# A GFNet and ReGLU block on one core: four buffers of rounded rows, a shorter first fetch, W_down's maxima later, and ScalarE's background work queued by units

## The chip, the cores and the metric

The kernel runs on one core of one Trainium2 chip. The metric is the time of one execution on the device in microseconds (us). Before the change three runs took 489.46 to 490.03 us, with a median of 489.92 us. What is asked is how this median moves.

## What is computed

The input x has S = 2048 rows of D = 448 numbers. A layer norm of each row feeds two branches, and their sum is added to x:

```python
xn = layernorm(x)                                  # over D, eps 1e-5
X  = rfft2(xn) * (w_r + 1j * w_i)                  # spectral branch
y  = irfft2(X, s=(S, D))
gate, up = xn @ W_gate, xn @ W_up                  # D x F, F = 1792
h  = where(gate > 0, gate, 0) * up
return x + y + h @ W_down                          # F x D
```

All arrays are in f32.

## The kernel before

TensorE works on fp16 operands. Each f32 operand is split in a rounded high part and a low part (the rest, rounded again), and a product of two such operands is three matmuls: high by high, high by low, low by high.

**Tiles and loops.** The hidden dimension F is cut in 14 *f-slices* of 128, in three groups of 5, 5 and 4. The rows are cut in four *chunks* q of 512, each of four *blocks* of 128 rows (block number n2 = q + 4j); the chunks are worked on in the order 0, 2, 1, 3. A *unit* `gu` (`gu_unit`) computes gate and up of one f-slice for one chunk: 20 full passes of 128x512 (L589, `gu_full`) and 4 half passes (L596, `gu_half`). The last 64 of the 448 input columns of gate and of up fill only half of TensorE's rows, so the half passes of two successive units (*mates*) stand together. Two units fit in PSUM (`gu`, two buffers). ScalarE and VectorE then make h from gate and up and split it (`gu_post`, L621 to L625). When the units of a group are done for a chunk, four `dn` follow, one for each block: 15 matmuls of 128x448 (12 in the last group), L637, two buffers in PSUM, each added to the output rows xy by VectorE (L643).

**Rows.** For each block the statistics of the layer norm are taken (`ln_stats`, L197 and L200) and the reciprocal deviations of a chunk's four blocks worked out together (`ln_rstd`, L208 to L214). `ln_xn` (L233) writes the normalized row xn, `ln_hi` (L242) rounds it into the buffer tt with two small copies on GpSimd, `ln_lo` (L254, L255) puts the low part beside it. Then tt is transposed into T, which the units read: in the opening by TensorE (`ln_tp`, L267) with the eviction `ln_ev` (L273 on ScalarE, L275 on VectorE), later by four transposing DMAs for each chunk (`ln_dma`, L261). There are two buffers tt, used in turn, and two of xn.

**Weights.** A *slab* is the gate half or the up half of one f-slice: 128x512 in f32, loaded by L175 into one of six buffers wst. `w_sq` takes its sum of squares (ScalarE, L525, then a sum over the partitions on GpSimd, L528), `w_scale` makes a power of two from it (VectorE, L537 to L541), and `w_hl` rounds the slab (ScalarE, L548) and takes the low part (VectorE, L549). W_down goes the same way for a whole group: `load_wd` (L185), `wd_max` (VectorE, L554, and GpSimd, L556), `wd_scale` (L563 to L570), `wd_split` (ScalarE, L575, and VectorE, L576).

**Order.** The opening is written by hand for TensorE, VectorE, ScalarE and SyncE (`manual_schedule`, L832 to L897): the loads of the first chunk's four blocks, seven slabs and the identity, chunk 0's layer norm, and f-slice 0 on the first half of the chunk's columns (blocks 0 and 4), then on the second half (blocks 8 and 12). Behind it a scheduler with a simulated timeline orders the instructions of each engine. Weight work hangs on units by the table `at`: `sched(gslot(s, n), ...)` puts a step n units ahead of the unit s. The spectral branch is a background list whose pieces are issued between units. What is issued with a unit may not be ordered ahead of an anchor, the last VectorE instruction of an earlier unit (`after`, `issue_after`). Each engine runs its instructions in the order so found, and SyncE (SP) issues all DMAs named here from one queue.

Of the kernel before, what the change touches and what calls it, by code (L numbers as in the profile page):

```python
# [116 lines left out]
def tile_gfnet_reglu(ctx: ExitStack, tc: tile.TileContext, x, xr, wgu, wd, wf, ident, c_fd, c_fm, c_im, c_id, out):  # L117
# [37 lines left out]
    def ft(shape, dt, name, bufs=1):  # L155
        return fwd_pool.tile(shape, dt, name=name, bufs=bufs)
# [8 lines left out]
    def load_xr(n2):  # L165

        xr_b[n2] = free.pop(0)
        xr_t[n2] = xr_b[n2].rearrange("p g c k -> p (g c k)")[:, 0:D]
        nc.sync.dma_start(xr_t[n2], xrv[:, n2, :])
# [9 lines left out]
    def load_wn(eng=nc.sync):  # L179
        if wq:  # L180
            load_w(*wq.pop(0), eng)
# [10 lines left out]
    mv = {}  # L192
# [8 lines left out]

    rst = {}

    def ln_rstd(q):
        w = ft([128, 6, 4], F32, "rs", 2)
        vv, r0, t, r, nm, sd = (w[:, i] for i in range(6))
        m = mv[q]
        A.activation(sd, m[:, :, 1], AF.Sqrt, bias=eps)  # L208
        V.tensor_scalar(vv, m[:, :, 1], 1e-5, None, op0=OP.add)
        V.reciprocal(r0, sd)  # L210
        V.scalar_tensor_tensor(t, r0, -0.5 * 2048, vv, op0=OP.mult, op1=OP.mult)
        V.tensor_tensor(t, t, r0, op=OP.mult)
        V.scalar_tensor_tensor(r, t, 1.5 * 2048, r0, op0=OP.add, op1=OP.mult)
        V.scalar_tensor_tensor(nm, m[:, :, 0], -1.0, r, op0=OP.mult, op1=OP.mult)  # L214
        for j in range(4):
            rst[q, j] = r[:, j:j + 1], nm[:, j:j + 1]

    xn, tt = {}, {}
    tts = [ft([128, 8, 128], F16, f"tt{i}") for i in range(2)]
    for t in tts:  # L220
        G.memset(t[:, 7, 48:64], 0.0)

    def new_tt(n2):
        tt[n2] = tts[state.setdefault("tn", 0) % 2]
        state["tn"] += 1

    def ln_xn(n2, act=True):
        xn[n2] = ft([128, D], F32, "xn", 2)
        r, nm = rst[n2 % 4, n2 // 4]
        if act:  # L230
            A.activation(xn[n2], xr_t[n2], AF.Identity, scale=r, bias=nm)
        else:
            V.tensor_scalar(xn[n2], xr_t[n2], r, nm, op0=OP.mult, op1=OP.add)  # L233
# [18 lines left out]
    def ln_lo(n2):  # L252
        x, t = xn[n2], tt[n2].rearrange("p a b -> p (a b)")
        V.tensor_tensor(t[:, 512:896], x[:, 0:384], t[:, 0:384], op=OP.subtract)  # L254
        V.tensor_tensor(t[:, 448:512], x[:, 384:448], t[:, 384:448], op=OP.subtract)  # L255

    tp, last = {}, {}

# [10 lines left out]
    def ln_ev(n2, a0, a1, act):  # L269
        q, j = n2 % 4, n2 // 4  # L270
        o = Tq[q][:, a0:a1, 128 * j:128 * (j + 1)]
        if act:
            A.activation(o, tp[n2][:, a0:a1], AF.Copy)  # L273
        else:
            last["V"] = V.tensor_copy(o, tp[n2][:, a0:a1]).ins  # L275

# [233 lines left out]


    wt, wdt, wsc = {}, {}, {}
    SMALL = V
    NR = max(GROUPS)


# [13 lines left out]
    def w_scale(f, gs=(0, 1)):  # L530
        m = state["wm", f]
        g = slice(gs[0], gs[-1] + 1)
        n = len(gs)
        sc = mt([128, 2, 2], F32, "wsc", 4)
        e = eg[:, f, g]
        E = SMALL
        E.tensor_scalar(e.bitcast(U32), m[:, 1, g].bitcast(U32), 1, EXPMASK, op0=OP.logical_shift_right,  # L537
                        op1=OP.bitwise_and)
        E.tensor_scalar(sc[:, 0, 0:n], e, TINY * SQ * 2.0 ** -64, 2.0 ** 50 / SQ, op0=OP.max, op1=OP.mult)
        V.reciprocal(sc[:, 1, 0:n], sc[:, 0, 0:n])  # L540
        E.tensor_scalar(e, e, TINY * SQ * 2.0 ** -64, 2.0 ** 64 / SQ, op0=OP.max, op1=OP.mult)  # L541
        for i, k in enumerate(gs):
            wsc[f, k] = sc[:, 1, i:i + 1]

# [73 lines left out]

    def gu_post(f, q):
        g1 = mt([128, 512], F32, "g1", 3)  # L620
        A.activation(g1, hps[f, q][:, 0, :], AF.Relu, scale=2.0 ** -22)  # L621
        last["V"] = V.scalar_tensor_tensor(g1, hps[f, q][:, 1, :], 2.0 ** -22, g1, op0=OP.mult, op1=OP.mult).ins  # L622
        h = ht[f, q] = mt([128, 2, 512], F16, "h", NR + 2)
        A.activation(h[:, 0, :], g1, AF.Copy)  # L624
        V.tensor_tensor(h[:, 1, :], g1, h[:, 0, :], op=OP.subtract)  # L625
# [167 lines left out]
    def sched(i, fn, *a):  # L793
        at.setdefault(max(i, -1), []).append((fn, a))
# [4 lines left out]
    def gslot(i, back):  # L799
        n = gpos[i] - back  # L800
        return gus[n] if n >= 0 else -1
# [11 lines left out]
            sched(gus[2 + 5 * c], load_x, q + 4 * j)  # L813
    for g, fs in enumerate(groups):
        s = max(i for i in gus if i < first["dn", g])
        sched(gslot(s, 5), wd_max, fs)
        sched(gslot(s, 3), wd_scale, g, fs)
        for i, f in enumerate(fs):
            sched(gslot(s, 3 - i // 2), wd_split, f, i)
        for f in (groups[g + 1] if g + 1 < len(groups) else ()):  # L820
            sched(s, load_wd, f)

# [9 lines left out]
    with tc.manual_schedule(engines={mybir.EngineType.PE, mybir.EngineType.DVE, mybir.EngineType.Activation,  # L832
                                     mybir.EngineType.SP}):
        A.activation(mt([128, 1], F32, "root"), eps, AF.Sqrt)
        for j in range(4):
            load_xr(4 * j)
        load_wn()
        load_wn()
        nc.sync.dma_start(id_t, ident)
        for _ in range(4):  # L840
            load_wn()
        G.memset(warm, 0.0)
        wps = psum.tile([128, 512], F32, name="dn", bufs=2)
        keep_warm(NWARM)
        for j in range(4):
            ln_stats(0, j)
        w_sq(0, (0,))
        ln_rstd(0)
        w_sq(0, (1,))
        for n2 in (0, 4):  # L850
            new_tt(n2)
        ln_hi(0, True)
        w_scale(0, (0,))
        ln_xn(0, False)
        ln_xn(4, False)
        ln_tp(0, (0, 1, 2))
        keep_warm(2)
        ln_lo(0)
        w_hl(0, 0)
        ln_hi(4)  # L860
        ln_tp(4, (0, 1, 2))
        keep_warm(2)
        ln_ev(0, 0, 3, True)
        ln_ev(4, 0, 3, True)
        ln_lo(4)
        gu_open(0, 0)
        gu_full(0, 0, (0,), half[0], True, False, seq1)
        ln_tp(0, (4, 5, 6, 3, 7))
        ln_tp(4, (4, 5, 6, 3, 7))
        w_scale(0, (1,))  # L870
        ln_ev(0, 3, 8, False)
        ln_ev(4, 3, 8, False)
        gu_full(0, 0, (0,), half[0], False, False, seq2)
        for n2 in (8, 12):
            new_tt(n2)
        ln_xn(12, False)
        w_hl(0, 1)
        ln_xn(8, True)
        ln_hi(8)
        gu_full(0, 0, (1,), half[0], True, False, seq1 + seq2)  # L880
        ln_lo(8)
        w_sq(1, (0,))
        ln_hi(12)
        w_sq(1, (1,))
        free.extend(xr_b.pop(4 * j) for j in range(4))
        ln_lo(12)
        ln_tp(8, (0, 1, 2, 4, 5, 6, 3, 7))
        w_scale(1)
        ln_ev(8, 0, 8, True)
        ln_tp(12, (0, 1, 2, 4, 5, 6, 3, 7))  # L890
        ln_ev(12, 0, 8, False)
        gu_full(0, 0, (0,), half[1], False, False, seq1 + seq2)
        w_hl(1, 0)
        w_hl(1, 1)
        gu_full(0, 0, (1,), half[1], False, False, seq1 + seq2)
        for j in range(4):
            load_xr(CHUNKS[1] + 4 * j)  # L897
# [10 lines left out]
    took = lambda u: 4.6 if u[0] == "gu" else 0.57 * len(groups[u[1]])  # L908
    nu = sum(took(u) for u in units[RAMP:]) - BGEND
    rate = nbg / nu  # L910
    anchors = [last["V"]]

    @contextmanager
    def after(i):
        with tc.issue_after(anchors[max(0, len(anchors) - 1 - i)]):
            yield

    for i, u in enumerate(units):
        is_gu = u[0] == "gu"
        if is_gu:  # L920
            _, g, f, q = u
            run_bg(until=marks["T", q])
            gu_unit(f, q, (mates.get(u) or (0, 0, None, None))[2:])
        else:
            _, g, n2, _ = u
            dn_mm(groups[g], n2)
        with after(LAG):
            for fn, a in at.get(i, []):
                with tc.high_priority(offset=200):
                    fn(*a)  # L930
            for v in units[i + 1:i + 1 + AHEAD]:
                if v[0] == "gu":
                    run_bg(until=marks["T", v[3]])
            run_bg(amount=took(u) * rate if i >= RAMP else 0.0)
        if is_gu:
            with tc.high_priority(offset=400):
                gu_post(f, q)
        else:
            if g == len(groups) - 1 and pos[0] < len(bg):
                run_bg(until=len(bg))  # L940
            with tc.high_priority(offset=400):
                dn_post(g, n2)
            if g == len(groups) - 1:
                store(n2)
        anchors.append(last["V"])
    run_bg(until=len(bg))


# [43 lines left out]
```

## Time and profile before

| | |
|---|---|
| median of three runs | 489.92 us |
| the profiled execution | 489.91 us |
| its span | 488.0 us |
| mean granted TensorE clock | 0.986 |
| TensorE busy | 468.8 us, 96% |
| VectorE busy | 383.7 us, 79% |
| ScalarE busy | 171.5 us, 35% |
| DMA | 38.71 MB in all |

The span is the time from the first to the last instruction of the core; all times in the trace count from its start. The engines are called PE (TensorE), DVE (VectorE), ACT (ScalarE), POOL (GpSimd) and SP (SyncE, which issues the DMAs); PEld is TensorE's loading of weights. A row such as `L589 MATMUL gu<-T,wt 128*128 128x512 f16 x20` names line, operation, the tile written, the tiles read, shape, type and count. The brackets at a row's end hold the idle time of the engine ahead of it and what ended it.

### The profile page before, as it was taken

The numbers are of one execution on the slowest core, as the hardware profiler recorded it, in microseconds if no ns is written. First come the engines' busy times: TensorE is split into PE (matmuls) and PEld (weight loads), VectorE is DVE, ScalarE is ACT, GpSimd is POOL, SyncE is SP. The second block draws the span as 40 slices with busy tenths as digits, with TensorE's granted clock in tenths as the row PEclk, the third lists the DMA queues.
The fourth block names the chain that finished last, engine by engine and source line by source line (L and its number), as shares of the span: only waits on it lengthen the run. The fifth ranks groups of instructions, "written<-read, shape, count | busy, mean of one in ns | idle before, by whom it ended". The sixth has DMA issues, their size and how long they took to land.

```text
span 488.0 us, 7692 instructions
## 1 busy us (share of the span) xinstructions
PE 468.8 (96%) x2896; PEld 245.3 (50%) x2896; DVE 383.7 (79%) x928; ACT 171.5 (35%) x340; POOL 26.4 (5%) x61
## 2 busy tenths in 40 slices
PE   6798599999999999999999999999999999999997
PEld 2543145555545555544444444444465655656653
DVE  5897149759893978999999999999999576776642
ACT  4768124322421764243023122262254234323310
POOL 1304000300200000000000000010000000000000
PEclk9899599999999999999999999999999999999999
DMA  7999400500510345432111102010000100010022
GB/s 258 385 375 251 89 0 18 118 17 4 122 29 0 122 123 174 133 107 91 39 40 43 35 19 59 24 40 1 0 23 24 60 12 21 23 69 32 21 75 95
DMA packets 35294, 38.71 MB, mean 79 GB/s; under 512 B 15302, under 2 KB 31430, under 8 KB 35256
## 3 DMA queue, kind: packets, MB, share of 16 engines
q1 hardware_dynamic: 35256, 38.21, 26.1%
q8 instruction: 23, 0.38, 0.3%
q14 instruction: 15, 0.12, 0.1%
HBM read 31.38 MB, written 3.67 MB: 72 GB/s over the span
## 4 chain that ended last, share of the span: by engine, by line
PE 75%; DVE 8%; DMA 5%; ACT 1%; issue 1%; POOL 0%; SPq 0%; ACTq 0%; DVEq 0%; POOLq 0%
PE gu L589 40%; PE dn L637 23%; PE fx L476 4%; PE fx L504 3%; PE gu L596 3%; DMA wmx<-in_wf 2%; DVE small L399 1%; PE fx L287 1%; DVE wt L549 1%; PE fx L329 1%; DMA T<-tt 1%; DMA fm<-in_c_fm 1%; PE fx L331 1%; PE fx L333 1%; DVE wdm L554 1%
## 5 line engine op out<-in xcount | busy, mean ns | idle before, releaser
L589 PE MATMUL gu<-T,wt 128*128 128x512 f16 (+1 forms) x1140 | 257.5, 379 | 1.7 <-DVE T L275 1.5
L589 PEld LDWEIGHTS <-wt 128*128 128x128 f16 x1140 | 110.1, 98 | 133.6 <-issue 15.0
L637 PE MATMUL dn<-wdt,h 128*128 128x448 f16 x672 | 135.8, 352 | 1.1 <-DVE xy L643 1.0
L637 PEld LDWEIGHTS <-h 128*128 128x128 f16 x672 | 65.5, 98 | 62.3 <-issue 2.4
L621 ACT ACTIVATE g<-gu 128x512 f32<-128x512 f32 x56 | 33.3, 594 | 98.4 <-PE gu L596 59.0
L622 DVE SCALAR_TENSOR_TENSOR g<-gu,g 128x512 f32<-128x512 f32 x56 | 38.4, 685 | 21.1 <-ACT g L621 20.8
L624 ACT ACTIVATE h<-g 128x512 f16<-128x512 f32 x56 | 35.1, 628 | 43.7 <-DVE g L622 43.2
L643 DVE SCALAR_TENSOR_TENSOR xy<-dn,dsc,xy 128x448 f32<-128x448 f32 x48 | 32.5, 680 | 20.5 <-PE dn L637 20.3
L625 DVE TENSOR_TENSOR h<-g,h 128x512 f16<-128x512 f32 x56 | 38.4, 686 | 7.9 <-ACT h L624 7.6
L463 DVE SCALAR_TENSOR_TENSOR vt<-y,fsc,vt 128x456 f16<-128x456 f32 x16 | 11.0, 691 | 18.6 <-ACT vt L457 18.6
L596 PE MATMUL gu<-T,wt 64*128 64x512 f16 x112 | 17.4, 390 | 8.1 <-DMA T<-tt 7.1
L548 ACT ACTIVATE wt<-wst,wsc 128x512 f16<-128x512 f32 x28 | 18.6, 711 | 16.7 <-DVE wsc L540 15.9
L476 PEld LDWEIGHTS <-vt 128*128 128x128 f16 x384 | 22.7, 98 | 3.4
L476 PE MATMUL fx<-im,vt 128*128 128x128 f16 x384 | 23.9, 219 | 0.0
L525 ACT ACTIVATE junk<-wst 128x512 bf16<-128x512 f32 x28 | 17.5, 623 | 17.7 <-DMA wst<-in_wgu 17.5
L457 ACT ACTIVATE vt<-y,fsc 128x456 f16<-128x456 f32 x16 | 10.8, 675 | 27.5 <-PE fx L476 22.5
L549 DVE SCALAR_TENSOR_TENSOR wt<-wst,wsc,wt 128x512 f16<-128x512 f32 x28 | 20.3, 743 | 0.0
L492 ACT ACTIVATE pgh<-pg 114x512 f16<-114x512 f32 x16 | 10.1, 630 | 27.9 <-DVE pg L490 27.9
L528 POOL PARTITION_ALL_REDUCE wm<-wm x16 | 8.7, 544 | 180.2 <-ACT junk L525 180.2
L504 PE MATMUL fx<-idc_t,pgh 114*128 114x112 f16 (+1 forms) x192 | 16.4, 236 | 0.0
L319 ACT ACTIVATE Xh<-X 128x456 f16<-128x456 f32 x16 | 9.1, 576 | 19.2 <-DVE X L317 12.2
L243 POOL COPY tt<-tt 128x48 f16<-128x48 f16 x16 | 10.8, 675 | 83.8 <-ACT tt L242 83.1
(102 smaller groups left out, 457.1 us busy)
## 6 DMA issues: line engine op xcount, KB each, us to landing
wst<-in_wgu SPq DMA_DIRECT2D x28, 256.0 KB, 4.7
wmx<-in_wf SPq DMA_DIRECT2D x16, 228.0 KB, 2.6
wf<-in_wf SPq DMA_DIRECT2D x16, 228.0 KB, 2.4
y<-in_xr SPq DMA_DIRECT2D x16, 224.0 KB, 4.8
xy<-in_x SPq DMA_DIRECT2D x16, 224.0 KB, 4.8
out<-xy SPq DMA_DIRECT2D x16, 224.0 KB, 1.9
wdst<-in_wd SPq DMA_DIRECT2D x14, 224.0 KB, 4.2
fm<-in_c_fm SPq DMA_DIRECT2D x16, 192.0 KB, 2.6
```

What stands on the lines that cost most here:

```text
L476: P.matmul(o, v[:, h, w], m[:, c, :], start=(i == 0), stop=(i == 5), skip_group_check=True)
L504: P.matmul(ps[:, o0:o1], h[:, a, i, :], idc_t[:, b, c0:c0 + o1 - o0], start=(j == 0 and i < 3), stop=True, skip_group_check=True)
L548: A.activation(w[:, 0:4, :], st, AF.Copy, scale=sc)
L549: V.scalar_tensor_tensor(w[:, 4:8, :], st, sc, w[:, 0:4, :], op0=OP.mult, op1=OP.subtract)
L589: last["P"] = P.matmul(hps[f, q][:, g, cs], wt[f, g][:, a, :], Tq[q][:, b, cs], start=(start and i == 0), stop=(stop and i == len(seq) - 1 ...
L596: m = P.matmul(hps[f, q][:, g, 0:512], wt[f, g][rows, 7, :], Tq[q][rows, b, :], start=start, stop=not start).ins
L621: A.activation(g1, hps[f, q][:, 0, :], AF.Relu, scale=2.0 ** -22)
L622: last["V"] = V.scalar_tensor_tensor(g1, hps[f, q][:, 1, :], 2.0 ** -22, g1, op0=OP.mult, op1=OP.mult).ins
L624: A.activation(h[:, 0, :], g1, AF.Copy)
L625: V.tensor_tensor(h[:, 1, :], g1, h[:, 0, :], op=OP.subtract)
L637: last["P"] = P.matmul(ps[:, 0:D], ht[f, q][:, a, js], wdt[f][:, b, :], start=(i == 0), stop=(i == n - 1)).ins
L643: last["V"] = V.scalar_tensor_tensor(xy[:, n2, :], dps[n2][:, 0:D], dsc[:, g:g + 1], xy[:, n2, :], op0=OP.mult, op1=OP.add).ins
```

## The change

- The buffers of rounded rows tt are four, used in turn. xn has no buffers of its own now; `ln_xn` takes one from the list `free` of the y buffers, and `ln_lo` gives it back.
- `ln_rstd` can work on some of a chunk's blocks (`js`), and its scratch tile rs has three buffers for two.
- The opening loads blocks 0 and 4, a slab, the identity, a slab, blocks 8 and 12, and four slabs; it takes statistics and rstd of blocks 0 and 4 first and those of 8 and 12 behind the first passes of f-slice 0; the square of the second slab is later, and both squares of f-slice 1 stand in one call.
- W_down's maxima, scales and splits are one unit later (for group 0 the maxima two).
- The anchors hold a ScalarE instruction also (`last["A"]`): what is issued with a unit may not be ordered ahead of the last ScalarE instruction of an earlier unit either.
- The alias SMALL of VectorE is gone; the instructions are the same.

```diff
-    def ln_rstd(q):
-        w = ft([128, 6, 4], F32, "rs", 2)
-        vv, r0, t, r, nm, sd = (w[:, i] for i in range(6))
-        m = mv[q]
+    def ln_rstd(q, js=(0, 1, 2, 3)):
+        n = len(js)
+        w = ft([128, 6, 4], F32, "rs", 3)
+        vv, r0, t, r, nm, sd = (w[:, i, 0:n] for i in range(6))
+        m = mv[q][:, js[0]:js[-1] + 1, :]
...
-    tts = [ft([128, 8, 128], F16, f"tt{i}") for i in range(2)]
+    tts = [ft([128, 8, 128], F16, f"tt{i}") for i in range(4)]
...
-        tt[n2] = tts[state.setdefault("tn", 0) % 2]
+        tt[n2] = tts[state.setdefault("tn", 0) % 4]
...
-        xn[n2] = ft([128, D], F32, "xn", 2)
+        xn_b[n2] = free.pop(0)
+        xn[n2] = xn_b[n2].rearrange("p g c k -> p (g c k)")[:, 0:D]
...
         V.tensor_tensor(t[:, 448:512], x[:, 384:448], t[:, 384:448], op=OP.subtract)
+        free.append(xn_b.pop(n2))
...
-            A.activation(o, tp[n2][:, a0:a1], AF.Copy)
+            last["A"] = A.activation(o, tp[n2][:, a0:a1], AF.Copy).ins
...
-        A.activation(g1, hps[f, q][:, 0, :], AF.Relu, scale=2.0 ** -22)
+        last["A"] = A.activation(g1, hps[f, q][:, 0, :], AF.Relu, scale=2.0 ** -22).ins
...
-        sched(gslot(s, 5), wd_max, fs)
-        sched(gslot(s, 3), wd_scale, g, fs)
+        sched(gslot(s, 4 if g else 3), wd_max, fs)
+        sched(gslot(s, 3 if g else 2), wd_scale, g, fs)
         for i, f in enumerate(fs):
-            sched(gslot(s, 3 - i // 2), wd_split, f, i)
+            sched(gslot(s, 2 - i // 2), wd_split, f, i)
...
-        for j in range(4):
-            load_xr(4 * j)
-        load_wn()
+        load_xr(0)
+        load_xr(4)
         load_wn()
         nc.sync.dma_start(id_t, ident)
+        load_wn()
+        load_xr(8)
+        load_xr(12)
...
-        for j in range(4):
-            ln_stats(0, j)
+        ln_stats(0, 0)
+        ln_stats(0, 1)
+        ln_rstd(0, (0, 1))
         w_sq(0, (0,))
-        ln_rstd(0)
-        w_sq(0, (1,))
...
         ln_tp(4, (4, 5, 6, 3, 7))
+        w_sq(0, (1,))
+        ln_stats(0, 3)
+        ln_rstd(0, (2, 3))
...
-        w_sq(1, (0,))
         ln_hi(12)
-        w_sq(1, (1,))
+        w_sq(1)
...
-    anchors = [last["V"]]
+    anchors, act_anchors = [last["V"]], [last["A"]]
...
-        with tc.issue_after(anchors[max(0, len(anchors) - 1 - i)]):
+        k = max(0, len(anchors) - 1 - i)
+        with tc.issue_after(anchors[k]), tc.issue_after(act_anchors[k]):
             yield
...
         anchors.append(last["V"])
+        act_anchors.append(last["A"])
```

The lines of the changed kernel lie a few numbers higher: L261 is L264 there, L525 is L527, L548 is L549, L549 is L550, L621 is L622, L624 is L625.

**Where instructions move.** SP, the loads around the gate slab of f-slice 4, before: it is wst_334, wst_332 is the up slab of f-slice 3, fm are tables of the spectral branch, y and xy are rows.

```order
L175 DMA wst_332<-in_wgu 128x512
L163 DMA xy_61<-in_x 128x448 x3
L189 DMA fm_768<-in_c_fm 128x768
L189 DMA fm_823<-in_c_fm 128x768
L169 DMA y8_74<-in_xr 128x448
L169 DMA y9_75<-in_xr 128x448
L169 DMA y10_76<-in_xr 128x448
L169 DMA y11_77<-in_xr 128x448
L163 DMA xy_61<-in_x 128x448 x2
L175 DMA wst_334<-in_wgu 128x512
```

The same place after; the gate slab of f-slice 4 is wst_341, the up slab of f-slice 3 wst_339.

```order
L163 DMA xy_61<-in_x 128x448 x4
L189 DMA fm_771<-in_c_fm 128x768
L189 DMA fm_826<-in_c_fm 128x768
L175 DMA wst_339<-in_wgu 128x512
L169 DMA y16_82<-in_xr 128x448
L169 DMA y4_70<-in_xr 128x448
L169 DMA y5_71<-in_xr 128x448
L169 DMA y7_73<-in_xr 128x448
L163 DMA xy_61<-in_x 128x448 x4
L169 DMA y6_72<-in_xr 128x448
L163 DMA xy_61<-in_x 128x448
L175 DMA wst_341<-in_wgu 128x512
```

From the start of the queue 39 loads stand ahead of the gate slab of f-slice 4 before, and 43 after; its up slab follows two rows later in both.

SP, the transposes of the second chunk, before (T2 is the transposed chunk, wdst are the slices of W_down of group 1):

```order
L175 DMA wst_480<-in_wgu 128x512
L261 DMA_TRANSPOSE T2_63<-tt0_96 128x8x128
L261 DMA_TRANSPOSE T2_63<-tt1_97 128x8x128
L185 DMA wdst_647<-in_wd 128x448
L185 DMA wdst_649<-in_wd 128x448
L185 DMA wdst_651<-in_wd 128x448
L185 DMA wdst_653<-in_wd 128x448
L185 DMA wdst_655<-in_wd 128x448
L261 DMA_TRANSPOSE T2_63<-tt0_96 128x8x128
L261 DMA_TRANSPOSE T2_63<-tt1_97 128x8x128
```

The same transposes after:

```order
L175 DMA wst_480<-in_wgu 128x512
L264 DMA_TRANSPOSE T2_63<-tt0_96 128x8x128
L264 DMA_TRANSPOSE T2_63<-tt1_97 128x8x128
L264 DMA_TRANSPOSE T2_63<-tt2_98 128x8x128
L264 DMA_TRANSPOSE T2_63<-tt3_99 128x8x128
L169 DMA y12_78<-in_xr 128x448
L185 DMA wdst_650<-in_wd 128x448
```

The four stand together, each with a buffer of its own, and the loads of W_down stand behind them.

ACT, around the rounding of f-slice 3's slabs, before (wst_330 and wst_332 are these slabs, wst_334 is the gate slab of f-slice 4):

```order
L624 ACTIVATE h_413<-g1_410 128x512
L548 ACTIVATE wt_392<-wst_330,wsc_372 128x512
L548 ACTIVATE wt_395<-wst_332,wsc_372 128x512
L621 ACTIVATE g1_446<-gu_383 128x512
L525 ACTIVATE junk_378,wm_377<-wst_334 128x512
L624 ACTIVATE h_449<-g1_446 128x512
```

And after, where wst_337 and wst_339 are f-slice 3's slabs and wst_341 the gate slab of f-slice 4:

```order
L625 ACTIVATE h_413<-g1_410 128x512
L622 ACTIVATE g1_446<-gu_390 128x512
L625 ACTIVATE h_449<-g1_446 128x512
L527 ACTIVATE junk_385,wm_384<-wst_341 128x512
L549 ACTIVATE wt_399<-wst_337,wsc_379 128x512
L549 ACTIVATE wt_402<-wst_339,wsc_379 128x512
```

The two roundings of f-slice 3 moved from ahead of the post work of the unit before to behind the square of f-slice 4's gate slab.

More of the change, by code (lines that the diff above doesn't have):

```diff
@@ L214, in ln_rstd @@
         V.scalar_tensor_tensor(nm, m[:, :, 0], -1.0, r, op0=OP.mult, op1=OP.mult)
-        for j in range(4):
-            rst[q, j] = r[:, j:j + 1], nm[:, j:j + 1]
-    xn, tt = {}, {}
-    tts = [ft([128, 8, 128], F16, f"tt{i}") for i in range(2)]
+        for i, j in enumerate(js):
+            rst[q, j] = r[:, i:i + 1], nm[:, i:i + 1]
+    xn, tt, xn_b = {}, {}, {}
+    tts = [ft([128, 8, 128], F16, f"tt{i}") for i in range(4)]
     for t in tts:
@@ L512, in tile_gfnet_reglu @@
     wt, wdt, wsc = {}, {}, {}
-    SMALL = V
     NR = max(GROUPS)
@@ L535, in w_scale @@
         e = eg[:, f, g]
-        E = SMALL
-        E.tensor_scalar(e.bitcast(U32), m[:, 1, g].bitcast(U32), 1, EXPMASK, op0=OP.logical_shift_right,
+        V.tensor_scalar(e.bitcast(U32), m[:, 1, g].bitcast(U32), 1, EXPMASK, op0=OP.logical_shift_right,
                         op1=OP.bitwise_and)
-        E.tensor_scalar(sc[:, 0, 0:n], e, TINY * SQ * 2.0 ** -64, 2.0 ** 50 / SQ, op0=OP.max, op1=OP.mult)
+        V.tensor_scalar(sc[:, 0, 0:n], e, TINY * SQ * 2.0 ** -64, 2.0 ** 50 / SQ, op0=OP.max, op1=OP.mult)
         V.reciprocal(sc[:, 1, 0:n], sc[:, 0, 0:n])
-        E.tensor_scalar(e, e, TINY * SQ * 2.0 ** -64, 2.0 ** 64 / SQ, op0=OP.max, op1=OP.mult)
+        V.tensor_scalar(e, e, TINY * SQ * 2.0 ** -64, 2.0 ** 64 / SQ, op0=OP.max, op1=OP.mult)
         for i, k in enumerate(gs):
@@ L844, in tile_gfnet_reglu @@
         keep_warm(NWARM)
-        for j in range(4):
-            ln_stats(0, j)
+        ln_stats(0, 0)
+        ln_stats(0, 1)
+        ln_rstd(0, (0, 1))
         w_sq(0, (0,))
-        ln_rstd(0)
-        w_sq(0, (1,))
         for n2 in (0, 4):
@@ L852, in tile_gfnet_reglu @@
         ln_hi(0, True)
+        ln_xn(0, False)
         w_scale(0, (0,))
-        ln_xn(0, False)
         ln_xn(4, False)
@@ L857, in tile_gfnet_reglu @@
         keep_warm(2)
+        w_hl(0, 0)
         ln_lo(0)
-        w_hl(0, 0)
         ln_hi(4)
+        ln_ev(0, 0, 3, True)
         ln_tp(4, (0, 1, 2))
         keep_warm(2)
-        ln_ev(0, 0, 3, True)
+        ln_stats(0, 2)
+        ln_lo(4)
         ln_ev(4, 0, 3, True)
-        ln_lo(4)
         gu_open(0, 0)
```

## The prediction

> **What bounds the kernel now.** I read the page first, then TensorE's waits, a table of windows, the chain of waits, and last the timeline of the two stretches in which TensorE stands.
>
> ```profile
> span 488.0 us, 7692 instructions
> PE 468.8 (96%) x2896; PEld 245.3 (50%) x2896; DVE 383.7 (79%) x928; ACT 171.5 (35%) x340; POOL 26.4 (5%) x61
> ```
>
> The profiled execution took 489.91 us around this span, the median of the three runs is 489.92, so its rows can be set against the median directly. TensorE is busy for 96%; the 19 us left are the opening and a few waits:
>
> ```profile
> PE gu L596 <- DMA T<-tt: 7.1, 1, 7.1
> PE gu L589 <- DVE T L275: 1.5, 2, 0.8
> PE gu L596 <- DVE wt L549: 1.1, 1, 1.1
> PE dn L637 <- DVE xy L643: 1.0, 1, 1.0
> ```
>
> The columns are total, count, longest. One wait stands out: 7.1 us for the transposed rows of the second chunk. Everything else this change could remove is near 1 us each. Windows (length, busy of PE, PEld, DVE, ACT, POOL, then the granted clock, the DMA share and GB/s) show what stands before and behind it:
>
> ```profile
> 24.00:33.00 9.00, 9.00 (x44) 3.95 (x44) 8.31 (x27) 5.78 (x12) 0.76 (x2) 1.00 1.05 380
> 40.00:42.00 2.00, 2.00 (x11) 0.87 (x9) 1.85 (x7) 1.35 (x3) 0.66 (x2) 1.00 1.22 251
> 42.00:44.00 2.00, 1.86 (x10) 0.87 (x9) 2.00 (x4) 2.00 (x4) 0.00 (x0) 1.00 1.35 162
> 50.00:52.00 2.00, 0.00 (x0) 0.00 (x0) 0.00 (x0) 0.00 (x0) 0.00 (x0) 0.50 1.17 160
> 58.00:60.00 2.00, 2.00 (x7) 0.75 (x6) 0.00 (x0) 0.00 (x0) 0.00 (x0) 0.57 0.00 0
> 221.00:300.00 79.00, 79.00 (x390) 35.80 (x389) 76.37 (x159) 17.54 (x36) 0.00 (x0) 1.00 0.15 44
> ```
>
> From 221 to 300 us TensorE doesn't pause, so what is gained before it is carried to the end. VectorE has only 2.6 us in 79 to spare there, but the change gives it no operation more in that stretch. From 24 to 33 us the loads fill the DMA engines: a load of 224 KB (229,376 bytes) at 380 GB/s takes 0.60 us. The chain gives the price of the wait:
>
> ```profile
> 49.30 4.75 DMA T<-tt
> 54.11 1.03 PE gu L596 x4
> 55.14 7.57 PE gu L589 x24
> 67.30 0.54 PE gu L596 x4
> 151.22 5.69 PE dn L637 x30
> 244.35 4.42 PE gu L589 x20
> ```
>
> At full clock a full pass takes 4.42/20 = 0.221 us, a dn matmul 5.69/30 = 0.19, four half passes 0.54. Behind the wait, 24 passes take 7.57 us and not 5.30, and the half passes 1.03: the clock, 0.50 while TensorE stands, costs another 2.27 + 0.49 = 2.8 us. Wait and cold clock are worth 9.9 us together.
>
> The timeline shows why the rows come late:
>
> ```profile
> 39.73 5.17 SPq L261 DMA_TRANSPOSE T<-tt  x2
> 42.04 5.00 PE L637 MATMUL dn<-wdt,h 128*128 128x448 f16 x24
> 45.40 2.31 SPq L185 DMA_DIRECT2D wdst<-in_wd  x5
> 46.27 0.56 ACT L242 ACTIVATE tt<-xn 128x448 f16<-128x448 f32 x1
> 47.34 0.56 ACT L242 ACTIVATE tt<-xn 128x448 f16<-128x448 f32 x1
> 47.88 4.14 SPq L261 DMA_TRANSPOSE T<-tt  x2
> ```
>
> There are two buffers tt. Blocks three and four of the chunk can be rounded (46.27 and 47.34) only once the first two transposes have landed, and five loads of W_down are issued between the pairs.
>
> **The change part by part.** *Four tt.* The order after shows all four transposes in one row, the W_down loads behind them. When do they land? The answers on the transposes (the instruction's own time on SP, min/median/max; then the time to landing; then the median to landing for the pair issued at 39.7 us, the pair at 47.9, and the four between 87 and 95):
>
> ```profile
> L261 SPq DMA_TRANSPOSE T<-tt x12: 1231/1246/3625, 39.7 to 132.3; - x12
> DMA to landing us min/median/max: 3.1/3.3/6.2
> T<-tt SPq DMA_TRANSPOSE x2, 6.0
> T<-tt SPq DMA_TRANSPOSE x2, 5.1
> T<-tt SPq DMA_TRANSPOSE x4, 3.2
> ```
>
> So SP issues one each 1.25 us, and it lands 3.3 us later when the engines have room. Between 50 and 52 us the engines have little but transposes to move, are full (1.17) and move 160 GB/s; four tiles of 262,144 bytes then take 6.6 us.
>
> [...]
>
> *The opening.* What decides when the fourth tile is ready is the stretch ahead of it.
>
> ```profile
> 20.16 2.36 PE L589 MATMUL gu<-T,wt 128*128 128x256 f16 x20 [0.81 <-DVE T L275]
> 23.58 0.60 PE L596 MATMUL gu<-T,wt 64*128 64x512 f16 x4 [1.07 <-DVE wt L549]
> 27.66 1.34 ACT L548 ACTIVATE wt<-wst,wsc 128x512 f16<-128x512 f32 x2 [1.10 <-DVE wsc L540]
> 30.80 0.63 ACT L525 ACTIVATE junk<-wst 128x512 bf16<-128x512 f32 x1 [1.32 <-DMA wst<-in_wgu]
> 31.34 0.19 ACT L525 ACTIVATION_READ_ACCUMULATOR junk<-wst 128x1 f32 x1
> 32.86 0.61 PE L596 MATMUL gu<-T,wt 64*128 64x512 f16 x4
> ```
>
> The first passes start earlier (two blocks and one slab are enough), but the second half of f-slice 0 needs blocks 8 and 12, and ACT has four squares (L525) ahead of their eviction; I leave it at 20.16. VectorE no longer has W_down maxima between the two low parts of f1's weights, which ends the 1.07 us wait at 23.58. TensorE comes to the half passes of f3 at 32.86 - 1.1 = 31.8. Splitting rstd adds six small VectorE operations ahead, hidden while TensorE waits for ACT.
>
> Against this stands a new stall. On SP the gate slab of f4 now has 43 loads ahead of it instead of 39: four more, 4 x 0.60 = 2.4 us, so it lands at about 33.2 and not 30.8. And on ACT the square of that slab now stands ahead of the rounding of f3's two slabs, which before ran at 27.66. ACT therefore holds f3's weights until 33.2 + 0.63 + 0.19 + 1.34 = 35.4, and the last low part ends one VectorE operation later (0.73, as in the row below), at 36.1. TensorE stands from 31.8 to 36.1, 4.3 us, about long enough for the clock to drop; I put 2.0 us on that, between nothing and the 2.8 above, near the dearer end because the idle is over half as long.
>
> ```profile
> 30.20 0.73 DVE L549 SCALAR_TENSOR_TENSOR wt<-wst,wsc,wt 128x512 f16<-128x512 f32 x1
> 38.92 0.55 DVE L254 TENSOR_TENSOR tt<-xn,tt 128x384 f16<-128x384 f32 x1
> 39.39 0.22 DVE L255 TENSOR_TENSOR tt<-xn,tt 128x64 f16<-128x64 f32 x1
> 40.62 0.49 DVE L233 TENSOR_SCALAR xn<-y,rs 128x448 f32<-128x448 f32 x1
> 41.98 3.07 DVE L576 SCALAR_TENSOR_TENSOR wdt<-wdst,wds,wdt 128x448 f16<-128x448 f32 x5
> ```
>
> From f3's half passes to the first dn took 42.04 - 32.86 = 9.2 us before; the same work after ends at 36.1 + 9.2 + 2.0 = 47.3. VectorE now does four xn (4 x 0.49) and four low parts (4 x 0.77) ahead of W_down's scales; laid end to end in the new order, with f4's weights ready at about 41.5, the fourth tile is ready at 44.6 and the splits (L576) begin at 46.5, the third ending at 48.4. The order now lets 14 dn matmuls go ahead of the chunk's half passes (24 before): 47.3 + 14 x 0.19 = 50.0. The transposes are issued from about 42.3 to 46.4. By landing time the last comes at 46.4 + 3.3 = 49.7, by the engines' rate at about 43.5 + 6.6 = 50.1. So three chains meet at about 50.1, with no idle long enough to cool the clock.
>
> *The sum.* Half passes at 50.1 instead of 54.1: 4.0 us. Ten dn matmuls still to do: minus 10 x 0.19 = 1.9. No cold clock behind: plus 2.8. Together 4.9 us, 489.9 - 4.9 = 485.0. Bounds: the half passes from 47.0 (no stall at f3) to 53.0 (one chain three late), which gives 482 to 488, and 490.7 if the clock then cools as before.
>
> [...]
>
> *The rest.* xn from the list of free y buffers costs nothing that I see (a buffer that is needed again soon would show as a late load). W_down's later splits and ACT's anchors move work in a stretch where ACT is busy 17.54 us of 79 and groups 1 and 2 need their W_down later than before; I put them at nothing, within -1 (the 1.0 us wait for xy goes) and +1 (a split one operation late).
>
> **The rivals.** *A, the slab is in time.* If f3 doesn't wait, TensorE reaches dn at 31.8 + 9.2 = 41.0, the rows land at about 47.0 and the gain is 7.1 - 1.9 + 2.8 = 8.0: 481.9. [...] Against: ACT works in order.
>
> *B, slower: the four transposes are bound by the DMA engines.* The first pair took from 39.73 to 47.3 at most (when the second buffer is written again), 7.6 us, the second from 47.88 to 54.1, 6.2 us. If four in a row take as long as both, the last lands at 42.3 + 13.8 = 56.1, TensorE stands from 50.0 and the clock cools again: half passes 2.0 us later than before and 1.9 us of dn still to do, with nothing saved in clock: 489.9 + 3.9 = 493.8. It decides against the change once the last transpose lands after about 52.2 with a cold clock (54.1 - 1.9), or 55 with a warm one. For it: shares of 1.35 at 162 GB/s. Against: loads in front of each pair were in those times, and 3.2 us at 87 us.
>
> *C, mostly eaten.* One of the three chains is 2 to 3 us late (the slab lands at 35 to 36, or VectorE's five extra maxima hold the rows): half passes at 53, gain 1.1 - 1.9 + 2.8 = 2.0, 487.9; with a short cold stretch 489 to 490.
>
> *D, it doesn't do what it says:* blocks three and four wait for a free y buffer, as they did for tt. The order shows four separate tiles and no load between, so this is only a small part of C.
>
> **How the numbers follow.** A measurement of this kernel can tell about 0.2%, 1.0 us. The forecast's own range, 483.5 to 487, has 0.56; A 0.14, C 0.18 (0.08 of it within 1.0 us of no change), B 0.12. So faster than 488.9: 0.56 + 0.14 + 0.10 = 0.80; same 0.08; slower than 490.9: 0.12. The range 481.5 to 489.5 leaves out B and the edges of A and C, together under 2 in 10.
>
> **What would show it.** In the profile after: the wait of L596 for T shrinks from 7.1 to under 2; a wait of L596 for VectorE's weights, about 4.3 us, appears near 32 to 36 with the clock at 0.50 behind it; the square of the f4 slab waits for its DMA until about 33; four transposes in a row from about 42; the half passes at about 50. The prediction is wrong if the f3 wait is missing (A), if the last transpose lands after 52 (B), or if TensorE has new waits after 100 us.

## The result, and the profile after

The changed kernel takes 483.83 us (median of 4 runs, 483.15 to 484.42) against 489.69 us for the kernel before beside it: a ratio of 0.988, with a 95% interval of 0.9863 to 0.9897. Measured again later it took 484.00 us, ratio 0.9893 (0.9876 to 0.9911). The forecast was 485.0 us, with a range of 481.5 to 489.5.

The profiled execution is the fastest of the four, 483.15 us, with this span and this busy time of TensorE:

```profile
span 481.2 us, 7678 instructions
PE 467.2 (97%) x2896; PEld 245.6 (51%) x2896; DVE 384.3 (80%) x934; ACT 170.3 (35%) x341; POOL 28.9 (6%) x62
```

TensorE's waits (total, count, longest) are other ones now:

```profile
PE gu L597 <- DVE wt L550: 4.0, 1, 4.0
PE gu L590 <- DVE T L278: 2.8, 1, 2.8
...
PE gu L590 <- DMA T<-tt: 0.4, 1, 0.4
PE gu L597 <- DMA T<-tt: 0.3, 1, 0.3
```

The 7.1 us for the second chunk's rows is 0.7 us in two pieces. In its place stands a wait of 4.0 us for f-slice 3's weights. (The 2.8 us wait is one in the opening, at 14.27 us; the opening as a whole is not longer, as the second half of f-slice 0 begins at 19.69 us and before at 20.16.) The timeline shows both ends of the wait for f3:

```profile
25.82 0.63 ACT L527 ACTIVATE junk<-wst 128x512 bf16<-128x512 f32 x1 [2.61 <-DMA wst<-in_wgu]
32.42 0.63 ACT L527 ACTIVATE junk<-wst 128x512 bf16<-128x512 f32 x1 [2.60 <-DMA wst<-in_wgu]
33.05 1.32 ACT L549 ACTIVATE wt<-wst,wsc 128x512 f16<-128x512 f32 x2
35.26 0.60 PE L597 MATMUL gu<-T,wt 64*128 64x512 f16 x4 [3.95 <-DVE wt L550]
35.80 10.49 PE L590 MATMUL gu<-T,wt 128*128 128x512 f16 x40
41.15 5.98 SPq L264 DMA_TRANSPOSE T<-tt  x4
46.13 2.81 PE L638 MATMUL dn<-wdt,h 128*128 128x448 f16 x14
49.22 0.61 PE L597 MATMUL gu<-T,wt 64*128 64x512 f16 x4 [0.29 <-DMA T<-tt]
49.76 4.49 PE L590 MATMUL gu<-T,wt 128*128 128x512 f16 x20
54.09 3.19 PE L638 MATMUL dn<-wdt,h 128*128 128x448 f16 x16
```

The square of f4's gate slab waits 2.60 us for its load, the two roundings of f3 stand behind it, and TensorE behind them. Then come four transposes in a row, 14 dn matmuls, and the second chunk's half passes at 49.22. The windows (length, busy of PE, PEld, DVE, ACT, POOL, clock, DMA share, GB/s) show the clock and the DMA engines:

```profile
36.00:38.00 2.00, 2.00 (x6) 0.71 (x5) 2.00 (x12) 1.60 (x3) 0.00 (x0) 0.52 1.00 254
38.00:40.00 2.00, 2.00 (x7) 0.80 (x6) 2.00 (x5) 2.00 (x6) 1.24 (x5) 0.63 0.92 256
44.00:46.00 2.00, 2.00 (x11) 0.94 (x10) 1.44 (x4) 1.78 (x4) 0.00 (x0) 1.00 1.12 198
48.00:50.00 2.00, 1.71 (x11) 0.56 (x10) 0.55 (x1) 0.13 (x1) 0.00 (x0) 1.00 0.97 265
```

The clock is cold behind f3's wait (0.52, 0.63) and full at the second chunk (1.00), where before it was 0.50 up to 58 us. With the 24th full pass of the second chunk and 30 dn matmuls done, the kernel before stands at 63.84 us (its chain). The changed one stands there at about 58.0: behind the 16 dn it goes on at 57.12, and four more passes of 0.22 us follow the 20. That is 5.9 us, as much as the whole change in the median. In the second profile of the changed kernel (an execution of 483.92 us) the same point comes at about 58.4 us, 5.4 us earlier than before. The first profile's span shows 0.9 us more than the 5.9; in it the wait for xy (1.0 us before) is gone, but the other three executions were 0.7 to 1.3 us longer than the profiled one.

### The profile page after: what moved, and what is told of

It reads as the page before. It is cut to its first block, busy times and chain, and to the rows that moved or that the text cites. A ratio compares the mean times of both kernels' runs of the same rounds, so it can differ in the third digit from the quotient of the medians.

```text
span 481.2 us, 7678 instructions
## 1 busy us (share of the span) xinstructions
PE 467.2 (97%) x2896; PEld 245.6 (51%) x2896; DVE 384.3 (80%) x934; ACT 170.3 (35%) x341; POOL 28.9 (6%) x62
## 4 chain that ended last, share of the span: by engine, by line
PE 80%; issue 8%; DMA 3%; DVE 2%; ACT 1%; SPq 1%; POOL 0%; POOLq 0%; ACTq 0%
PE gu L590 42%; PE dn L638 24%; PE fx L479 4%; PE fx L507 3%; PE gu L597 3%; PE fx L290 2%; DMA T<-tt 2%; PE fx L332 1%; DMA wst<-in_wgu 1%; PE fx L334 1%; PE fx L336 1%; ACT wt L549 1%; SPq L264 1%; DVE wdm L555 1%; DVE wt L550 0%
## 5 line engine op out<-in xcount | busy, mean ns | idle before, releaser
L622 ACT ACTIVATE g<-gu 128x512 f32<-128x512 f32 x56 | 33.3, 595 | 119.2 <-PE gu L597 70.3
L623 DVE SCALAR_TENSOR_TENSOR g<-gu,g 128x512 f32<-128x512 f32 x56 | 38.4, 685 | 23.0 <-ACT g L622 22.9
L625 ACT ACTIVATE h<-g 128x512 f16<-128x512 f32 x56 | 35.0, 626 | 37.6 <-DVE g L623 35.3
L644 DVE SCALAR_TENSOR_TENSOR xy<-dn,dsc,xy 128x448 f32<-128x448 f32 x48 | 32.4, 679 | 18.1 <-PE dn L638 18.1
L549 ACT ACTIVATE wt<-wst,wsc 128x512 f16<-128x512 f32 x28 | 18.9, 712 | 13.3 <-DVE wsc L541 11.8
L550 DVE SCALAR_TENSOR_TENSOR wt<-wst,wsc,wt 128x512 f16<-128x512 f32 x28 | 20.4, 745 | 3.4 <-ACT wt L549 3.4
L527 ACT ACTIVATE junk<-wst 128x512 bf16<-128x512 f32 x28 | 17.4, 622 | 6.1 <-DMA wst<-in_wgu 5.8
L530 POOL PARTITION_ALL_REDUCE wm<-wm x15 | 7.3, 485 | 160.0 <-ACT junk L527 160.0
L344 DVE TENSOR_TENSOR y<-y,y 128x456 f32<-128x456 f32 x22 | 13.9, 630 | 0.5
```

What stands on the lines that cost most here:

```text
L549: A.activation(w[:, 0:4, :], st, AF.Copy, scale=sc)
L550: V.scalar_tensor_tensor(w[:, 4:8, :], st, sc, w[:, 0:4, :], op0=OP.mult, op1=OP.subtract)
L622: last["A"] = A.activation(g1, hps[f, q][:, 0, :], AF.Relu, scale=2.0 ** -22).ins
L644: last["V"] = V.scalar_tensor_tensor(xy[:, n2, :], dps[n2][:, 0:D], dsc[:, g:g + 1], xy[:, n2, :], op0=OP.mult, op1=OP.add).ins
```

## The experiments

Each run has its own runs of the kernel before beside it, and each ratio is to those; the times of before were 489.2 to 490.3 us. To compare two variants I compare their ratios.

**Two buffers again.** All of the change but the two more buffers.

```diff
-    tts = [ft([128, 8, 128], F16, f"tt{i}") for i in range(4)]
+    tts = [ft([128, 8, 128], F16, f"tt{i}") for i in range(2)]
...
-        tt[n2] = tts[state.setdefault("tn", 0) % 4]
+        tt[n2] = tts[state.setdefault("tn", 0) % 2]
```

> The changed kernel with two buffers tt again, all else as changed (the order now puts two transposes, loads, one transpose, loads, one transpose). Theory (the third and fourth transpose have to wait for a buffer): TensorE waits 5 to 8 us for the second chunk's rows again, and the time is 488 to 491 us. Rival (the new opening and the later W_down bring the gain, the buffers only cover what is hidden anyway): within 1 us of the changed kernel's 483.8.

488.07 us, ratio 0.9964 (0.9945 to 0.9982). From its timeline, ScalarE's roundings into tt, the transposes and the half passes of the second chunk:

```profile
36.22 1.04 ACT L244 ACTIVATE tt<-y 128x448 f16<-128x448 f32 x2 [0.63 <-DVE y L235]
38.94 3.81 SPq L264 DMA_TRANSPOSE T<-tt  x2
43.97 0.58 ACT L244 ACTIVATE tt<-y 128x448 f16<-128x448 f32 x1 [1.25 <-DMA T<-tt]
45.45 1.26 SPq L264 DMA_TRANSPOSE T<-tt  x1
49.50 1.35 SPq L264 DMA_TRANSPOSE T<-tt  x1
53.77 0.96 PE L597 MATMUL gu<-T,wt 64*128 64x512 f16 x4 [3.50 <-issue]
```

The third rounding waits for a transpose, the second chunk starts at 53.77 and not 49.22, though the first two transposes go out earlier than in the changed kernel. The theory holds in its cause; the wait is 3.5 us and not 5 to 8 (TensorE comes later), and the bracket names no releaser for it; the last transpose goes out at 49.50. In the kernel before the same wait leaves no idle time on ScalarE, which squares slabs up to the third rounding; but there too the two roundings stand right behind the landings of the first two transposes (landed at 45.97 and 46.99, rounded from 46.27 and 47.34). Without the buffers the other parts are worth 1.8 us; on top of them the buffers bring 3.5 to 4.1 (ratio 0.9964 against 0.9893 and 0.988).

**The loads of W_down behind the transposes.** The kernel before, with one order forced on SP (`add_manual_dep` without a semaphore, as the kernel uses it for its half passes).

```diff
+        last["T", q] = nc.sync.dma_start_transpose(...).ins
...
+        if f in groups[1]:
+            tc.add_manual_dep(ld, last["T", 2].name, NOSYNC, reason="behind the transposes")
```

> The kernel before, still with two buffers tt, but the loads of W_down of group 1 stand behind all four transposes of the second chunk on SP. Theory (buffers): the third tile can't be rounded before the first has landed, the loads in between are only a part; the last transpose lands 1 to 2 us earlier, 487.5 to 489.5 us. Rival (loads in front): the wait shrinks to under 3 us and the time to 484 to 486.

488.46 us, ratio 0.9978 (0.9964 to 0.9992), about 1.1 us less than before. Its timeline (the profile is of an execution of 489.42 us):

```profile
40.47 11.05 SPq L263 DMA_TRANSPOSE T<-tt  x4
47.00 0.56 ACT L244 ACTIVATE tt<-xn 128x448 f16<-128x448 f32 x1
53.74 1.04 PE L599 MATMUL gu<-T,wt 64*128 64x512 f16 x4 [5.96 <-DMA T<-tt]
```

Nothing stands between the transposes, and still the third rounding is at 47.00 and the wait 5.96 us. The buffers made the wait; the loads were a small part.

**Four buffers alone.** The kernel before with four tt and xn from the y buffers: the changed kernel with the opening, W_down's units and the anchors of before.

> The kernel before with the four buffers tt and xn from the y buffers alone: opening, W_down's times and anchors as before. Theory (the buffers bring nearly all, and the wait at f3 is the price of the other parts): no wait at f3, a wait of up to 3 us at f4's weights, 482 to 486 us. Rival (the opening or W_down's later maxima are needed for the gain): 487 to 490.

486.11 us, ratio 0.9917 (0.9891 to 0.9942). From the timeline of TensorE:

```profile
33.51 0.61 PE L597 MATMUL gu<-T,wt 64*128 64x512 f16 x4
39.94 0.39 PE L590 MATMUL gu<-T,wt 128*128 128x512 f16 x1 [1.40 <-ACT wt L549]
41.56 5.96 PE L590 MATMUL gu<-T,wt 128*128 128x512 f16 x19 [1.24 <-DVE wt L550]
51.24 0.61 PE L597 MATMUL gu<-T,wt 64*128 64x512 f16 x4
```

No wait at f3, waits of 1.4 and 1.2 us at f4's weights, and none for the rows. By the ratio the buffers alone are worth about 4 us. The rest of the change brings 1 to 2 us on top, though the intervals overlap; the run with two buffers, where the other parts alone brought 1.8 us, says the same. So the theory's "nearly all" was too much.

**W_down's units, the anchors, the opening, one at a time.** Each is the changed kernel with one part as before.

```diff
-        sched(gslot(s, 4 if g else 3), wd_max, fs)
+        sched(gslot(s, 5), wd_max, fs)
...
-        with tc.issue_after(anchors[k]), tc.issue_after(act_anchors[k]):
+        with tc.issue_after(anchors[k]):
...
-        load_xr(0)
-        load_xr(4)
+        for j in range(4):
+            load_xr(4 * j)
```

> The changed kernel with W_down's maxima, scales and splits at their old units. The order then has f-slice 3 rounded ahead of f4's squares again, and f4's two slabs later still (47 and 48 loads ahead); the first unit of the second chunk stands ahead of all dn matmuls. Theory (what counts is when the second chunk's rows and f4's weights come, and whether dn matmuls stand ahead to fill the time): no wait at f3, a wait of 3 to 5 us at f4's weights, another for the rows with a cold clock behind it: 486 to 489 us. Rival (the place of W_down's steps doesn't matter): 483 to 484.5.

486.76 us, ratio 0.9943 (0.9931 to 0.9956). Its timeline:

```profile
34.33 0.61 PE L597 MATMUL gu<-T,wt 64*128 64x512 f16 x4
43.29 0.39 PE L590 MATMUL gu<-T,wt 128*128 128x512 f16 x1 [3.94 <-ACT wt L549]
50.04 0.60 PE L597 MATMUL gu<-T,wt 64*128 64x512 f16 x4
```

No wait at f3, 3.94 us at f4 as expected; the further wait for the rows didn't come, since TensorE was held until they had landed. So later maxima of W_down are worth over 2 us here, although they bring the wait at f3.

> The changed kernel without the ScalarE anchors. The order is nearly the same up to the second chunk (f5's squares stand further ahead, 18 dn matmuls for 14). Theory (the anchors have no part in the gain): 483 to 485 us, the wait at f3 still about 4 us. Rival (they keep ScalarE free for h and the splits): 486 or more, with waits of TensorE for ScalarE or for h.

485.14 us, ratio 0.9911 (0.9897 to 0.9925), with a wait of 2.8 us at f3. It lies just above what was expected and about 1 us over the changed kernel; the intervals overlap, so whether the anchors give anything stays open.

> The changed kernel with the opening of before. The order then puts four loads of W_down between the two pairs of transposes, though all four buffers are there, and has f4's second square too ahead of f3's rounding. Theory (the opening as such saves 1 us, the rest comes by where the loads fall): the wait at f3 is 3 to 5 us, the rows come 2 to 3 us later than in the changed kernel: 485.5 to 488.5 us. Rival (the opening gives nothing that lasts): 483 to 485.

486.19 us, ratio 0.9933 (0.9919 to 0.9947): 2.0 to 2.6 us of the gain go with the opening. Four loads of W_down stand between the pairs of transposes here, and TensorE waits 4.72 us for the rows:

```profile
53.09 1.03 PE L597 MATMUL gu<-T,wt 64*128 64x512 f16 x4 [4.72 <-DMA T<-tt]
```

The wait at f3 is 2.3 us, less than the 3 to 5 expected, and the rows come 3.9 us later than in the changed kernel.

**f-slice 3 first.** The wait of 4.0 us taken away in the changed kernel: ScalarE may square f4's slabs only behind the rounding of f3.

```diff
-            sched(gslot(s, 5), w_sq, f)
+            sched(gslot(s, 4 if f == 4 else 5), w_sq, f)
...
+            if f == 4:
+                tc.add_manual_dep(sq, last["hi", 3].name, NOSYNC, reason="f3 is rounded first")
```

> The changed kernel with one order forced: ScalarE squares f-slice 4's slabs only behind the rounding of f-slice 3. Theory (the 4.0 us wait of f3's half passes and the cold clock behind it lie on the path): that wait goes, part of it comes back at f4's weights, the second chunk starts 1 to 3 us earlier, 481 to 483 us. Rival (the four transposes set the second chunk, whatever TensorE did before): 483.3 to 484.5.

487.03 us, ratio 0.9942 (0.9921 to 0.9963): slower than the changed kernel by 2.4 to 3 us, which neither theory had. Its timeline, of the slowest of nine executions (488.43 us, the fastest took 485.21):

```profile
32.90 0.61 PE L599 MATMUL gu<-T,wt 64*128 64x512 f16 x4 [1.50 <-DVE wt L552]
38.59 4.64 SPq L264 DMA_TRANSPOSE T<-tt  x2
40.43 4.27 PE L592 MATMUL gu<-T,wt 128*128 128x512 f16 x19 [2.00 <-DVE wt L552]
43.34 1.40 SPq L175 DMA_DIRECT2D wst<-in_wgu  x2
44.54 1.83 PE L640 MATMUL dn<-wdt,h 128*128 128x448 f16 x8
44.85 2.74 SPq L264 DMA_TRANSPOSE T<-tt  x2
50.16 1.04 PE L599 MATMUL gu<-T,wt 64*128 64x512 f16 x4 [3.79 <-DMA T<-tt]
```

TensorE is 2.4 us earlier at f3, but the rows land no earlier (50.0, and 49.1 in the changed kernel), only 8 dn matmuls stand ahead of them for 14, and TensorE waits 3.79 us with a cold clock behind (0.50 from 50 to 56 us): the half passes take 1.04 us for 0.61. So taking the wait away in this way brings nothing. That it costs nothing by itself is not shown, since the forced order moved more than the squares: the fourth tile is ready at 41.75, but two loads of slabs now stand on SP between the pairs of transposes (43.34), and the second pair goes out behind them, at 44.85. What the changed kernel's own trace shows is that two chains end together at 49 us: TensorE's dn matmuls end at 48.94, and the rows let it go on at 49.22. An earlier TensorE alone would have waited for the rows.

**The rows first.** So I shortened the other: the second chunk's layer norm is issued right behind the opening, f4's slabs are loaded ahead of rows that are needed later, the slabs of f5 to f7 behind the transposes.

```diff
+    with tc.high_priority(offset=1000):
+        run_bg(until=marks["T", 2])
...
+        if 5 <= f < 8:
+            tc.add_manual_dep(ld, last["T", 2].name, NOSYNC, reason="behind the transposes")
...
+        if n2 % 4 % 2:
+            tc.add_manual_dep(ld, last["W4"].name, NOSYNC, reason="behind the slabs of f4")
```

> The changed kernel with the order around the second chunk forced: its layer norm is issued right behind the opening, f4's slabs are loaded ahead of the rows of chunks 1 and 3, and the slabs of f5 to f7 behind the four transposes. Theory (the second chunk's rows set the time, as the run with f-slice 3 first showed, and they are late because of f4's slab, the squares and loads that stand ahead of them): rows landed at 42 to 45 us and not 49.1, no wait at f3, 477 to 482 us. Rival (the transposes are bound by the DMA engines or by GpSimd's copies, so TensorE only waits longer for them and cools): 484 to 488.

485.76 us, ratio 0.9935 (0.9916 to 0.9953). The wait for the rows is gone, but the wait at f3 is 5.0 us:

```profile
30.65 0.63 ACT L535 ACTIVATE junk<-wst 128x512 bf16<-128x512 f32 x1 [3.75 <-DMA wst<-in_wgu]
37.74 1.03 PE L605 MATMUL gu<-T,wt 64*128 64x512 f16 x4 [5.00 <-DVE wt L558]
```

f4's squares stood ahead of f3's rounding on ScalarE still, with slabs that stood behind three loads of the spectral branch on SP; the first square waits 3.75 us. On VectorE the four xn stand ahead of f3's low parts too. The time is the rival's, but not its reason: the four transposes went out from 38.58 us, the last landed at 46.6 (42 to 45 expected), and the wait moved to weights.

The second try puts f4's squares behind f3's rounding too, as in the run with f-slice 3 first, and its slabs ahead of those loads. The changed kernel ran beside it.

> The run with the rows first, mended by what it showed: f4's squares stand behind f3's rounding on ScalarE, and f4's slabs are loaded ahead of the tables of the spectral branch too. Theory (each wait of TensorE between 30 and 50 us comes from a step that stands in its engine's queue behind another that still waits for a load): rows landed at about 42 us, the wait at f3 under 1.5 us, at f4's weights under 2 us, 14 dn matmuls ahead of the second chunk, 478 to 482 us. Rival (VectorE has no more room in this stretch, so the wait moves to f4's weights or to W_down's splits and the clock cools there): 484 to 487.

> The changed kernel itself on the same chip as the run with the rows first, as a base: 483 to 485 us.

484.31 us, ratio 0.9892 (0.9875 to 0.9909), against 484.00 and 0.9893 for the changed kernel. From its timeline, VectorE between 28 and 36 us and what waits for it:

```profile
28.30 1.13 DVE L566 TENSOR_REDUCE wdm<-wdst 128x1 f32<-128x448 f32 x2
29.42 1.66 DVE L566 TENSOR_REDUCE wdm<-wdst 128x1 f32<-128x448 f32 x3
32.55 1.77 DVE L242 TENSOR_SCALAR y<-y,rs 128x448 f32<-128x448 f32 x4
34.84 1.40 DVE L561 SCALAR_TENSOR_TENSOR wt<-wst,wsc,wt 128x512 f16<-128x512 f32 x2
36.30 0.61 PE L608 MATMUL gu<-T,wt 64*128 64x512 f16 x4 [3.35 <-DVE wt L561]
36.84 10.49 PE L601 MATMUL gu<-T,wt 128*128 128x512 f16 x40
```

The four transposes go out from 37.07 us, 4 us earlier than in the changed kernel. The last lands at 45.3, not at the expected 42, but the rows don't hold TensorE now. What holds it is f3 again, this time by VectorE: five maxima of W_down (2.8 us) and four xn (1.8 us) stand ahead of f3's scales and low parts. So the time is the rival's, and so is the engine, but the wait stayed at f3. Here the 3.35 us do lie on the path, as the next two runs show.

**The maxima behind f4, and without them.** The last pair: the second try with the maxima forced behind f4's low parts; and the second try without the maxima of group 0.

```diff
+            if f < 5:
+                tc.add_manual_dep(r, last["lo", 4].name, NOSYNC, reason="behind f4")
```

> The second run with the rows first, with W_down's five maxima forced behind the low parts of f-slice 4 on VectorE (the order then puts the whole first unit of the second chunk ahead of the dn matmuls). Theory (VectorE's queue sets f3's weights now, and the maxima, 2.8 us, stand ahead of them): the wait at f3 falls from 3.3 to under 2 us, with no cold clock behind it, and 1 to 2 us come back at f4's weights: 481 to 483.5 us. Rival (the same work of VectorE only changes places, the wait with it): 484 to 486.

> The second run with the rows first, leaving out the five maxima of W_down's group 0 (a constant stands in their place, so W_down's scales are not the right ones). Theory (VectorE has no room between 27 and 42 us): 2.8 us of its work less give 1.5 to 3.5 us, 481 to 483 us. Rival (TensorE is held there by loads or by ScalarE): within 1 us of the 484.3 with the maxima.

481.69 us, ratio 0.9829 (0.9804 to 0.9855), and 481.00 us, ratio 0.981 (0.9789 to 0.9831). The timeline of the first:

```profile
33.88 0.61 PE L610 MATMUL gu<-T,wt 64*128 64x512 f16 x4 [0.94 <-DVE g L636]
34.01 8.21 SPq L271 DMA_TRANSPOSE T<-tt  x4
34.42 8.94 PE L603 MATMUL gu<-T,wt 128*128 128x512 f16 x40
44.09 0.60 PE L610 MATMUL gu<-T,wt 64*128 64x512 f16 x4 [0.72 <-DMA T<-tt]
44.62 4.49 PE L603 MATMUL gu<-T,wt 128*128 128x512 f16 x20
```

40 passes take 8.94 us and not 10.49, so hardly any clock is lost (it was 1.00 from 32 to 52 us), and the second chunk starts at 44.09 (its first unit stands ahead of the dn matmuls in this order). Both theories held in their cause, only that nothing came back at f4's weights, and that by the ratios leaving the maxima out is worth about 4 us, more than the 3.5 named. In their new place the maxima cost about 0.7 us by the medians, with intervals that overlap. The version with the maxima behind f4 is 0.5 to 0.65% faster than the changed kernel and 1.7% than the one before, with all of the computation.

## Why the prediction was right

**The four buffers.** The step was that the third and fourth tile wait for a buffer, and that with four the transposes go out 1.25 us apart and land 3.3 us later. After, they were issued from 41.15 to 45.9, against 42.3 to 46.4 forecast, and SP was done with them at 47.13; the median to landing was 3.3 us, and the second chunk began at 49.22 against 50.1. Three runs show the cause: the changed kernel with two buffers loses 3.5 to 4.1 us (second chunk at 53.77), the kernel before with four gains about 4, and with the loads behind and two buffers 5.96 us of wait are left.

**The new wait at f3.** The forecast had 4.3 us, the trace has 3.95, by the steps named: f4's slab late (32.4 us, 33.2 forecast: four more loads made it 1.6 us later and not 2.4), ScalarE in order. Its cold clock was put at 2.0 us; the clock was 0.52 from 36 to 38 us, and 40 passes took 10.49 us for the 8.81 that 40 took before, so 1.7. The slab and the clock add up to dn at 46.13, where 47.3 was forecast: two small errors, both to one side. TensorE's coming to f3 (31.3 us, 31.8 forecast) made the wait longer, not dn later. So the second chunk came 0.9 us earlier than forecast, which is most of the 1.2 us between 485.0 and 483.83.

**The sum.** The half passes came 4.9 us earlier (4.0 forecast), ten dn matmuls were still to do, and the cold clock of 2.8 us behind the old wait is gone, as forecast: 4.9 - 1.9 + 2.8 = 5.8, measured 5.9.

**Rival A was wrong about the rows.** It had 481.9 us if f3 didn't wait, by letting the rows land at 47.0 then. In the three runs in which f3 waits less or not at all (f-slice 3 first, four buffers alone, W_down's units as before) the last transpose landed at 50.0, 50.6 and 48.8 us, against 49.1 in the changed kernel, and the times were 486 to 487. The rows don't follow TensorE there; they follow the queues of SP, VectorE and ScalarE. A time near A's was reached only by shortening both chains (481.69).

**Rival B** (the transposes bound by the DMA engines) is out at its price: the four took 8 us from the first issue to the last landing and not 13.8 (10 in the version with the maxima behind f4, from 34.01), with the engines at 1.12 and 198 GB/s from 44 to 46 us. At that share little room seems left in that step, by my estimate.

**The rest.** "W_down's later splits and ACT's anchors ... at nothing" was wrong for W_down: with its old units the time is 2.4 to 3.1 us longer, and TensorE waits 3.94 us for f4's weights. The forecast counted their effect only through f3. On the opening it was right in kind: the second half of f-slice 0 starts at 19.69 (20.16 kept) and the wait for f1's low part is gone. Taking the whole opening back cost 2.0 to 2.6 us, about twice the 1.1 named, with loads between the transposes again. Four buffers tt with two of xn were not run.

## What to carry to other kernels

A wait that ends just when another chain would have made the engine wait anyway may have no price: before removing it, look what is late next, and shorten both. And a forced order moves more than the step it names, so look at the other queues before reading the time. In these traces ScalarE works through its queue in order, and a step that needs a load not yet landed holds back what is ready behind it (2.60 us at the square of f4's slab, so that f3's rounding began at 33.05 us; with f3 first it began at 30.60); put ready work that TensorE needs first. And to take away a wait can be worth more than its length, where the clock falls behind it (7.1 us of waiting and 2.8 us of clock here).

## What the runs showed of the hardware

In these runs the clock's price didn't follow the length of the wait. A wait of 7.1 us cost 2.8 us of clock; 3.79 us in the run with f3 first cost as much (half passes 1.04 us for 0.61, 20 passes 6.82 for 4.42), and 3.95 us in the changed kernel 1.7. Two waits of 1.40 and 1.24 us close together, in the run with four buffers alone, also cost 1.8 (19 passes in 5.96 us, 4.2 at the full clock's 0.221). The 0.94 and 0.72 us of the version with the maxima behind f4 cost next to nothing (40 passes in 8.94 us for 8.81). Nor did the clock fall a fixed time after the stop: in the kernel before TensorE stops at 47.04 us and the clock is 0.50 from 50 us on; in the changed kernel it stops at 31.31, and the clock is still 1.00 from 35 to 36 us and 0.52 from 36 to 38.

GpSimd's copies of 48 columns took from 0.22 to 2.61 us in the changed kernel. In its timeline stand

```profile
39.67 2.61 POOL L245 COPY tt<-tt 128x48 f16<-128x48 f16 x1
43.56 0.22 POOL L245 COPY tt<-tt 128x48 f16<-128x48 f16 x1
```

The long one belongs to the third tile, whose transpose goes out only at 44.49, so it held nothing back. (The second transpose is issued 1.9 us behind the first and not 1.25; the trace doesn't name what held it.) VectorE was busy around both, but on different operations: beside the long one mostly on those that read two tiles from SBUF (L550, L256, L257), beside the short one on L623, which reads one of its two from PSUM. In these traces every copy into tt of over 0.6 us (0.61 to 4.16 us) lies for most of its time beside operations of the first kind, though some short ones (0.23 us) do too. Whether that slows the copies wasn't tried.
